# One-core attention with two mixture-of-experts layers: decay sums spread by GpSimd, first block's bias on TensorE, first keys on another queue

## Chip, cores and metric

The kernel runs on 1 core of one Trainium2 chip. The metric is the device time of one execution in microseconds (us), the median of repeated runs. Engines: PE is TensorE (matmuls; PEld its weight loads), DVE is VectorE, ACT is ScalarE, POOL is GpSimd, SP is SyncE. SPq and ACTq are the DMA-issuing instructions of those engines.

## What is computed

Causal attention with a decay bias, then two expert layers, all in fp32:

```python
B, H, S, D = 2, 8, 576, 64
scores = q @ k.T / sqrt(D)
cum = cumsum(log(clip(f, 1e-4, 1)), axis=-1)
scores = where(causal, -1e9, scores + cum[:, :, :, None] - cum[:, :, None, :])
attn = softmax(scores) @ v
x = moe_top1(attn as 1152 rows of 512)
out = moe_top2(x)
```

The query's own sum `cum[..., None]` is the same for a whole row of the softmax and drops out; the kernel adds only the key's part, the negated sum, which every query row (so every partition) needs.

## The kernel before, in words

**Stages.** `phase_a` is the attention with the routing of the first expert layer (to about 132 us of the span), `moe1` and `moe2` are the expert layers, eight experts of two matrices each.

**Units of the attention.** A batch's 576 rows are cut into chunks of 64, 128, 128, 128, 128 rows (CHUNKS, L39). Units are numbered batch times 5 plus chunk; the two 64-row chunks (units 0 and 5) are worked as one unit, 0, with batch 0 in partitions 0 to 63 and batch 1 in 64 to 127. ORDER (L38) is 0, 1, 2, 3, 4, 6, 7, 8, 9. Each unit has four steps, one for each pair of heads, so step n = 0 to 3 is unit 0, 4 to 7 unit 1, 8 to 11 unit 2, 12 to 15 unit 3, 16 to 19 unit 4, 20 to 23 unit 6. `first[i]` and `last[i]` are a unit's first and last step.

**A step (loop at L550).** `qk` writes the scores of two heads into two PSUM banks: three matmuls a head (hi times hi, hi times lo, lo times hi; L255), and for all units but 0 one bf16 matmul a head that puts -1e9 above the diagonal (L258). DVE then adds the decay bias from SBUF (tile WB, or Wd for unit 0), negates and takes the minimum, in one instruction a head and column group (L265), and ACT takes the exponential (L273). Then follow `warm` (1 to 4 filler matmuls of 512 columns in steps 0 to 15, L562), `trans` of the step two before, what is registered as `mid`, `pvmm` of the step three before, the rest of `trans`, and what is registered as `todo`. `at(n, fn)` registers work with a step; `prep` always goes to `mid`.

**`prep(i)`** transposes a unit's keys and queries on PE into a PSUM bank (L214), ACT writes the hi part (L222) and DVE the lo part (L223). For units above 0 the bank is the single one of `ppk`, for keys and queries alike. Unit 1 is prepared whole in step 1, each other unit's keys in step first-4 and its queries in step first-3.

**The decay sums.** `decay` (L112) ends in tile `ncs`: the negated sums, 128 partitions of 72 values, partition (b*8+h)*8+j. ACT's queue writes them to DRAM as `ncum` (L130), and SP's queue reads them back with a partition step of 0, so that all 128 partitions of WB hold them (`load_w`, L196 to L199): seven loads, 4.7 MB into SBUF. Unit 0 has its own way: `bcast_w` (L179) makes 32 small matmuls of a column of the identity with `ncs`, and DVE adds the mask (L189) into Wd, whose off-diagonal blocks `clear_w` set to -1e9.

**Order.** PE and SP run in program order (`manual_schedule`, L1254) in the attention; ACT, DVE and POOL are ordered by the tile scheduler there. In the expert layers all engines run in program order. SP issues q, k, v, WB, zero-fill and weight DMAs from one queue, in order; a DMA whose data or buffer isn't ready holds all behind it.

**Expert 0's second half (`moe1`, L966).** In each of its eight `ffn2` steps f, expert 1's next weight block is split (ACT hi, L813; DVE lo, L821), and in steps 4 and 6 the two row blocks of expert 1's input are transposed and split (`xsplit`, L867 to L874).

Of the kernel before, what the change touches and what calls it, by code (L numbers as in the profile page):

```python
# [18 lines left out]
P = 128  # L19
# [34 lines left out]
def consts(g):  # L54
# [13 lines left out]
    g.mask = g.ap.tile([P, P], F32, tag="mask", name="mask")  # L68
    nc.vector.tensor_scalar(g.mask, mp, 0.0, NEG, op0=ALU.is_gt, op1=ALU.mult)
# [3 lines left out]
    nc.vector.tensor_scalar(g.nid, mp, 0.0, NEG, op0=ALU.is_equal, op1=ALU.mult)  # L73
    g.ones = cp.tile([P, P], BF16, tag="ones", name="ones")
# [37 lines left out]
def decay(g, f):  # L112
    nc, cp = g.nc, g.cp
    W = B * H * S // P
    fl = g.fl
    nc.vector.tensor_scalar(fl, fl, 1e-4, 1.0, op0=ALU.max, op1=ALU.min)
    a = g.ap.tile([P, W], F32, tag="cma", name="cma")
    tot = cp.tile([P, 1], F32, tag="tot", name="tot")
    nc.scalar.activation(a, fl, AF.Ln, accum_out=tot)
    pt = g.ptr.tile([P, 4, P], "pt")  # L120
    nc.tensor.transpose(pt[:W, 0, :], a, g.ident)
    at = g.ap.tile([W, P], F32, tag="at", name="at")
    nc.vector.tensor_copy(at, pt[:W, 0, :])
    po = g.pxx.tile([P, 512], "po")
    nc.tensor.matmul(po[:, :W], g.seg, tot.to_broadcast([P, W]), start=True, stop=False)
    nc.tensor.matmul(po[:, :W], at, g.tri[:W, :W], start=False, stop=True)
    g.nc_sb = cp.tile([P, W], F32, tag="ncs", name="ncs")
    nc.vector.tensor_scalar(g.nc_sb, po[:, :W], -1.0, None, op0=ALU.mult)
    g.ncum = g.dp.tile([B, H, S], F32, tag="ncum", name="ncum")
    nc.scalar.dma_start(bass.AP(tensor=g.ncum.tensor, offset=g.ncum.offset, ap=[[W, P], [1, W]]), g.nc_sb)  # L130
# [5 lines left out]
def phase_a(g, q, k, v, f, wg, noise, out):  # L136
# [3 lines left out]
    qn, kn, vt, WB, Wd = {}, {}, {}, {}, {}  # L140

    def load_qk(i):
        b, c = units[i]
        s0, r = CHUNKS[c]
        for src, dst, nm in ((q, qn, "qn"), (k, kn, "kn")):
            t = ap.tile([P, DM], F32, tag=nm, name=nm, bufs=2)
            for bb, o in ((0, 0), (1, 64)) if i == 0 else ((b, 0),):
                nc.sync.dma_start(t[o:o + r].rearrange("p (h d) -> p h d", h=H), src[bb, :, s0:s0 + r, :].rearrange("h p d -> p h d"))
            dst[i] = t
# [29 lines left out]
    def bcast_w():  # L179
        w = Wd[0]  # L180
        pp = g.psc.tile([P, 4, P], "pw")
        pw = pp.rearrange("p a w -> p (a w)").rearrange("p (h w) -> p h w", h=H)
        for h in range(H):
            for b in range(B):
                o = (b * H + h) * 8
                nc.tensor.matmul(pw[64 * b:64 * b + 64, h, :], g.ident[:, o:o + 1].to_broadcast([P, 64]), g.nc_sb[:, :64], start=True, stop=True)
        for b in range(B):
            m = slice(64 * b, 64 * b + 64)
            nc.vector.tensor_tensor(w[m, :, m], pw[m], g.mask[m, None, m].to_broadcast([64, H, 64]), op=ALU.add)  # L189

    def clear_w():
        w = Wd[0] = ap.tile([P, H, P], F32, tag="Wd", name="W0", bufs=1)
        nc.gpsimd.memset(w[:64, :, 64:], NEG)
        nc.gpsimd.memset(w[64:, :, :64], NEG)
# [9 lines left out]
    def prep(i, half=None):  # L204
# [31 lines left out]
    def qk(i, p):  # L236
# [23 lines left out]
        for hh in range(2):  # L260
            for n, (a0, a1) in enumerate(cols):
# [4 lines left out]
                    out=ts[hh][:r, a0:a1], in0=ps[hh][:r, :a1 - a0], in1=WB[b][:r, h, a0:a1] if i else Wd[0][:r, h, :r], op0=ALU.add, op1=ALU.min,  # L266
# [231 lines left out]
    clear_w()  # L498
# [15 lines left out]
    at(2, load_w, 0, 192, 576)  # L514
    for i in ORDER[1:]:
# [34 lines left out]
    for n in range(len(work) + LAG + 9):  # L550
# [11 lines left out]
        if n < 16:  # L562
# [277 lines left out]
def moe1(g, x_rows, w1, w2, wg2, wn2):  # L840
# [102 lines left out]
    for e in range(E):  # L943
# [356 lines left out]
```

## Time and profile before

| what | us |
|---|---|
| median of 3 runs | 557.39 (556.54 to 559.33) |
| the profiled execution | 556.42 |
| its span, first to last instruction | 554.6 |
| PE busy | 538.9 (97%) |
| DVE busy | 327.4 (59%) |
| ACT busy | 262.4 (47%) |
| POOL busy | 109.3 (20%) |

The profiled execution's own time is 1.8 us more than its span and 1.0 us less than the median. Matmuls are pipelined and their ends are modelled: a busy PE can still be waiting, and one matmul's duration is longer than the distance to the next. A row of the timeline gives start, duration, engine, line, operation, output and inputs, and in brackets how long the engine had been idle and who released it. A row of the chain of waits gives start, duration and what was on the path that ended last.

### The profile page before, as it was taken

What the parts mean: (1) busy time and instruction counts of PE and PEld (TensorE: products, weight loads), DVE (VectorE), ACT (ScalarE), POOL (GpSimd) and SP (SyncE); (2) the same over time, 40 slices, a digit from 0 to 9 for tenths busy, and PEclk for the clock granted to TensorE, in tenths of its full rate; (3) what the DMA queues carried; (4) which work ended last, traced back from release to release, by engine and by line L of the source; (5) the groups of instructions that cost most, each with busy time, mean ns of one, the idle gap of its engine ahead of it and who ended that gap; (6) DMA issues with size and microseconds to landing.
All of it is one profiled execution on the core that took longest, in us unless ns stands there. A gap on an engine that the chain in (4) does not pass through costs nothing.

```text
span 554.6 us, 11866 instructions
## 1 busy us (share of the span) xinstructions
PE 538.9 (97%) x4292; PEld 505.7 (91%) x4292; DVE 327.4 (59%) x1094; ACT 262.4 (47%) x661; POOL 109.3 (20%) x169
## 2 busy tenths in 40 slices
PE   7899999999999999999999999999999999999994
PEld 4577787788989999999999999999999999999993
DVE  4578778875256374233238766757576666666642
ACT  3566767672265455222225445445454545454510
POOL 5010001111000311320223600222213130314032
PEclk9999999999999999999999999999999999999998
DMA  6798979753998856877884299866777667642021
GB/s 147 210 230 232 332 258 262 263 197 109 308 355 285 283 172 219 260 231 247 269 244 146 69 365 372 220 198 203 186 211 216 212 203 211 182 119 64 19 67 44
DMA packets 103874, 116.80 MB, mean 211 GB/s; under 512 B 38205, under 2 KB 73053, under 8 KB 103808
## 3 DMA queue, kind: packets, MB, share of 16 engines
q1 hardware_dynamic: 97136, 99.86, 59.8%
q0 software_dynamic: 6528, 16.06, 8.8%
q8 instruction: 36, 0.59, 0.4%
q14 instruction: 30, 0.25, 0.1%
q10 hardware_dynamic: 144, 0.04, 0.0%
HBM read 91.63 MB, written 25.85 MB: 212 GB/s over the span
## 4 chain that ended last, share of the span: by engine, by line
PE 87%; DVE 5%; DMA 3%; SPq 3%; issue 1%; ACT 1%; POOL 0%; POOLq 0%; ACTq 0%
PE ps L1061 19%; PE py L1072 19%; PE py L907 12%; PE psn L885 5%; PE ps L895 4%; PE sc L255 3%; PE pt L296 3%; PE pv L324 3%; PE pyr L635 2%; PE px L361 2%; PE pv L319 2%; PE pyr L1094 2%; DMA wr<-in_moe_w_dram 2%; PE ps L896 2%; PE pt L1030 1%; PE warm L101 1%
## 5 line engine op out<-in xcount | busy, mean ns | idle before, releaser
L821 DVE TENSOR_TENSOR wlo<-wr,whi 128x512 fp32r<-128x512 f32 x152 | 103.2, 690 | 26.7 <-ACT whi L813 24.2
L1061 PE MATMUL ps<-X,whi 128*128 128x312 f32 (+4 forms) x512 | 110.2, 306 | 0.0
L1072 PE MATMUL py<-H,whi 128*128 128x312 f32 (+4 forms) x512 | 109.7, 305 | 0.0
L813 ACT ACTIVATE whi<-wr 128x512 fp32r<-128x512 f32 x152 | 93.0, 625 | 29.5 <-PE py L1072 22.7
L1061 PEld LDWEIGHTS ps<-X,whi 128*128 128x128 f32 x512 | 83.5, 189 | 0.1
L1072 PEld LDWEIGHTS py<-H,whi 128*128 128x128 f32 x512 | 83.4, 188 | 0.0
L907 PE MATMUL py<-H,wr 128*128 128x192 f32 (+7 forms) x512 | 80.9, 314 | 0.0
L1072 PE MATMUL py<-H,wlo 128*128 128x312 f32 (+4 forms) x256 | 77.4, 302 | 0.0
L1061 PE MATMUL ps<-X,wlo 128*128 128x312 f32 (+4 forms) x256 | 77.4, 302 | 0.0
L907 PEld LDWEIGHTS py<-H,wr 128*128 128x128 f32 x512 | 76.0, 190 | 0.8
L692 POOL DMA_INDIRECT x<-yr,sl x30 | 34.5, 1149 | 132.5 <-ACT Xn L871 45.4
L1097 POOL DMA_INDIRECT out_dram<-ot,tk x24 | 27.4, 1140 | 148.2 <-DVE ot L1096 147.9
L1063 ACT ACTIVATE H<-ps 128x312 fp32r<-128x312 f32 (+4 forms) x64 | 27.2, 424 | 60.3 <-PE ps L1061 60.3
L273 ACT ACTIVATE pr<-t,nmax 128x192 f32<-128x192 f32 (+4 forms) x72 | 41.9, 584 | 25.9 <-DVE nmax L265 25.6
L1065 DVE SCALAR_TENSOR_TENSOR H<-ps,H 128x312 fp32r<-128x312 f32 (+4 forms) x64 | 30.4, 475 | 30.9 <-ACT H L1063 30.9
L1061 PEld LDWEIGHTS ps<-X,wlo 128*128 128x128 f32 x256 | 48.2, 188 | 0.0
L1072 PEld LDWEIGHTS py<-H,wlo 128*128 128x128 f32 x256 | 48.1, 188 | 0.0
L885 PE MATMUL psn<-Xn,wr 128*128 128x192 f32 (+4 forms) x320 | 46.8, 298 | 0.0
L885 PEld LDWEIGHTS psn<-Xn,wr 128*128 128x128 f32 x320 | 44.2, 190 | 0.2
L265 DVE CUSTOM_DVE_ANT_0 t<-sc,WB 128x192 f32<-128x192 f32 (+3 forms) x64 | 28.6, 478 | 6.3 <-PE sc L258 4.2
L895 PE MATMUL ps<-X,whi 128*128 128x480 f32 (+2 forms) x96 | 31.3, 382 | 0.7 <-DVE X L874 0.7
L1047 POOL DMA_INDIRECT pv<-out_dram,tk x21 | 23.1, 1101 | 35.1 <-DMA out_dram<-ot,tk 20.6
(271 smaller groups left out, 818.5 us busy)
## 6 DMA issues: line engine op xcount, KB each, us to landing
wr<-in_moe_w_dram SPq DMA_DIRECT2D x128, 512.0 KB
xs<-z SPq DMA_DIRECT2D x18, 264.0 KB
x<-z SPq DMA_DIRECT2D x16, 258.0 KB
WB<-ncum SPq DMA_DIRECT2D x4, 576.0 KB
out_dram<-z SPq DMA_DIRECT2D x9, 256.0 KB
qn<-in_q_dram SPq DMA_DIRECT2D x8, 256.0 KB
kn<-in_k_dram SPq DMA_DIRECT2D x8, 256.0 KB
x2g<-x SPq DMA_DIRECT2D x3, 628.9 KB
```

What stands on the lines that cost most here:

```text
L265: nc.vector.tensor_tensor_reduce(out=ts[hh][:r, a0:a1], in0=ps[hh][:r, :a1 - a0], in1=WB[b][:r, h, a0:a1] if i else Wd[0][:r, h, :r], op0= ...
L273: nc.scalar.activation(dst, src, AF.Exp, bias=nmax[:r, h:h + 1], scale=-1.0, accum_out=rsum[:r, h:h + 1])
L692: d = nc.gpsimd.indirect_dma_start(out=g.x2, out_offset=bass.IndirectOffsetOnAxis(ap=sl[:T, t, kk:kk + 1], axis=0), in_=yr[:T, t], in_offs ...
L813: self.g.nc.scalar.activation(self.hi[u], self.g.stream.view(self.base + u), AF.Copy)
L821: self.g.nc.vector.tensor_tensor(self.lo[u], self.g.stream.view(self.base + u), self.hi[u], op=ALU.subtract)
L885: nc.tensor.matmul(ps[:, :C], w[:, d, :], X[e][:, d, :], start=d == 0, stop=d == KD - 1)
L895: nc.tensor.matmul(ps[:, :2 * C], hi[:, d, :], X[e][:, d, :], start=d == 0, stop=False)
L907: nc.tensor.matmul(py[dd][:, :C], w[:, dd, :], H[e][:, f, :], start=f == 0, stop=f == KF - 1)
L1061: nc.tensor.matmul(ps[:, :C], w[:, d, :], X[e][:, x, d, :], start=d == 0 and i == 0, stop=d == KD - 1 and i == 2)
L1065: nc.vector.scalar_tensor_tensor(H[e][:, 1, f, :], ps[:, :C], 0.0, H[e][:, 0, f, :], op0=ALU.max, op1=ALU.subtract)
L1072: nc.tensor.matmul(py[dd][:, :C], w[:, dd, :], H[e][:, x, f, :], start=f == 0 and i == 0, stop=f == KF - 1 and i == 2)
L1097: d = nc.gpsimd.indirect_dma_start(out=out, out_offset=bass.IndirectOffsetOnAxis(ap=tok[:T, t:t + 1], axis=0), in_=ot[:T], in_offset=None, ...
```

## The change

- `bcast_w`, `clear_w`, the mask tile and the DRAM tile `ncum` go. For unit 0, `qk` adds the key's sums with four small fp32 matmuls (two heads, two batches) and the mask with two bf16 matmuls straight into the score banks; DVE's L265 adds a tile of zeros instead of Wd.
- `load_w(b)` is one DMA on ACT's queue from 64 partitions of `ncs` to one row (partition 0) of WB. `spread_w` copies a part of that row to all 128 partitions with GpSimd's `partition_broadcast`: four spreads of two heads by 192 columns ahead of step 0, four of two heads by 384 columns in steps 0 to 3, and for batch 1 four of two heads by 576 columns in steps 6, 8, 10 and 12.
- Unit 0's keys are loaded by ACT's queue instead of SP's.
- In `prep`, unit 1's queries are transposed into a bank of `ptr` instead of the single bank of `ppk`; where there are two parts (unit 0's keys), both hi parts are written before the lo parts.
- From unit 2 on, keys are prepared in step first-5 (was first-4) and q and k are loaded in first-9 (was first-8).
- The filler matmuls of steps 12 to 15 go.
- Expert 1's input is transposed in steps 2 and 5 of expert 0's `ffn2` (was 4 and 6).

```diff
@@ consts
-    g.mask = g.ap.tile([P, P], F32, tag="mask", name="mask")
-    nc.vector.tensor_scalar(g.mask, mp, 0.0, NEG, op0=ALU.is_gt, op1=ALU.mult)
...
+    g.far = g.ap.tile([P, P], BF16, tag="far", name="far")
+    nc.vector.tensor_scalar(g.far, mp, 0.0, None, op0=ALU.is_gt)
+    nc.vector.memset(g.far[64:, :64], 1.0)
@@ decay
-    g.ncum = g.dp.tile([B, H, S], F32, tag="ncum", name="ncum")
-    nc.scalar.dma_start(bass.AP(tensor=g.ncum.tensor, offset=g.ncum.offset, ap=[[W, P], [1, W]]), g.nc_sb)
@@ phase_a
+    zero = ap.tile([P, P], F32, tag="zero", name="zero")
+    nc.gpsimd.memset(zero, 0.0)
@@ load_qk
-                nc.sync.dma_start(t[o:o + r]...
+                (nc.sync if i or src is q else nc.scalar).dma_start(t[o:o + r]...
@@ bcast_w, clear_w: removed
-    def load_w(b, c0, c1, h0=0, h1=H):
-        if b not in WB:
-            WB[b] = ap.tile([P, H, S], F32, tag="WB", name="WB", bufs=2)
-        nc.sync.dma_start(WB[b][:, h0:h1, c0:c1], bass.AP(tensor=g.ncum.tensor, ...
+    def load_w(b):
+        WB[b] = ap.tile([P, H, S], F32, tag="WB", name="WB", bufs=2)
+        nc.scalar.dma_start(WB[b][0:1].rearrange("a h s -> a (h s)"), g.nc_sb[64 * b:64 * b + 64])
+
+    def spread_w(b, c0, c1, h0, h1):
+        w = WB[b][:, h0:h1, c0:c1]
+        nc.gpsimd.partition_broadcast(w, w[0:1])
@@ prep
-            pt = (g.ppk if i else g.ptr).tile([P, 4, P], "pk")
+            pt = (g.ppk if i > 1 or i and isk else g.ptr).tile([P, 4, P], "pk")
...
             for hi, lo, pv in parts:
                 nc.scalar.activation(hi, pv, AF.Copy, scale=sc)
+            for hi, lo, pv in parts:
                 nc.vector.scalar_tensor_tensor(lo, pv, sc, hi, op0=ALU.mult, op1=ALU.subtract)
@@ qk
-            if i and a1 == w:
+            if i == 0:
+                for hh in range(2):
+                    for x in range(B):
+                        o, m = (x * H + 2 * p + hh) * 8, slice(64 * x, 64 * x + 64)
+                        nc.tensor.matmul(ps[hh][m, m], g.ident[:, o:o + 1].to_broadcast([P, 64]), g.nc_sb[:, :64], start=False, stop=False)
+                for hh in range(2):
+                    nc.tensor.matmul(ps[hh][:, :P], g.nid, g.far, start=False, stop=True)
+            elif a1 == w:
...
-                    ... in1=WB[b][:r, h, a0:a1] if i else Wd[0][:r, h, :r], ...
+                    ... in1=WB[b][:r, h, a0:a1] if i else zero, ...
@@ the plan
-    bcast_w()
     warm(g, 4, g.psc)
-    load_w(0, 0, 192, 0, 4)
-    load_w(0, 0, 192, 4, 8)
+    load_w(0)
+    for j in range(4):
+        spread_w(0, 0, 192, 2 * j, 2 * j + 2)
...
-    at(2, load_w, 0, 192, 576)
+    for j in range(4):
+        at(j, spread_w, 0, 192, 576, 2 * j, 2 * j + 2)
+    at(4, load_w, 1)
...
-            at(n - 4, prep, i, 0)
+            at(n - 5, prep, i, 0)
             at(n - 3, prep, i, 1)
...
-                at(max(n - 8, 0), load_qk, i)
+                at(max(n - 9, 0), load_qk, i)
...
-        at(first[6] - 9 + 2 * j, load_w, 1, 0, 576, 2 * j, 2 * j + 2)
+        at(6 + 2 * j, spread_w, 1, 0, 576, 2 * j, 2 * j + 2)
...
-        if n < 16:
+        if n < 12:
             warm(g, (4, 4, 4, 2)[n] if n < 4 else 1, g.psc)
@@ moe1
-                if f == (0 if e else 4):
+                if f == (0 if e else 2):
                     xsplit(e + 1, 0)
-                if f == (3 if e else 6):
+                if f == (3 if e else 5):
                     xsplit(e + 1, 1)
```

## Rows read from the trace of the kernel before

**Rows 1.** The page, part 1 (busy time) and the path's shares by engine.

```profile
PE 538.9 (97%) x4292; PEld 505.7 (91%) x4292; DVE 327.4 (59%) x1094; ACT 262.4 (47%) x661; POOL 109.3 (20%) x169
...
PE 87%; DVE 5%; DMA 3%; SPq 3%; issue 1%; ACT 1%; POOL 0%; POOLq 0%; ACTq 0%
```

**Rows 2.** Busy time by stretch: us, PE, PEld, DVE, ACT, POOL, PEclk, DMA, GB/s.

```profile
10.00:20.00 10.00, 7.82 (x59) 4.88 (x58) 5.09 (x23) 4.83 (x19) 0.00 (x0) 1.00 0.76 167
...
40.00:50.00 10.00, 10.00 (x104) 7.62 (x100) 7.99 (x33) 5.76 (x20) 0.00 (x0) 1.00 0.92 249
...
60.00:70.00 10.00, 9.51 (x115) 7.73 (x114) 8.46 (x38) 7.63 (x20) 0.00 (x0) 1.00 1.04 331
```

**Rows 3.** Timeline, the first fillers, keys' DMA, ACT's logarithm, unit 0's key transposes.

```profile
1.07 3.87 PE L101 MATMUL warm<-ones 128*128 128x512 bf16 x10 [1.07 <-DVE ohs L845]
...
2.65 1.32 SPq L148 DMA_DIRECT2D kn<-in_k_dram  x2
...
2.88 0.26 ACT L119 ACTIVATE cma<-fl 128x72 f32<-128x72 f32 x1 [0.84 <-DVE fl L116]
...
6.89 0.63 PE L214 MATMUL pk<-ident,kn 128*128 128x128 f32 x4 [1.02 <-DMA kn<-in_k_dram]
```

**Rows 4.** Timeline, unit 0's bias and its first scores; a later mask pair.

```profile
7.89 1.15 PE L186 MATMUL pw<-ncs,ident 128*64 128x64 f32 x32
...
11.38 1.02 PE L101 MATMUL warm<-ones 128*128 128x512 bf16 x4 [0.77 <-DVE W L189]
...
12.33 0.55 PE L255 MATMUL sc<-kT,qT 64*128 64x128 f32 x6
...
20.30 0.28 PE L258 MATMUL sc<-stri,nid 128*128 128x128 bf16 x2
```

**Rows 5.** Timeline, unit 1's preparation and its first scores; unit 2's.

```profile
15.70 0.66 PE L214 MATMUL pk<-ident,qn 128*128 128x128 f32 x4 [1.41 <-DVE kT L223]
...
19.79 0.58 PE L255 MATMUL sc<-kT,qT 64*128 64x192 f32 x6
...
23.55 0.66 PE L214 MATMUL pk<-ident,qn 128*128 128x128 f32 x4 [0.56 <-DVE kT L223]
```

**Rows 6.** Timeline, PE at 57 to 65 us.

```profile
57.56 1.40 PE L255 MATMUL sc<-kT,qT 64*128 64x288 f32 x12
...
61.34 1.06 PE L255 MATMUL sc<-kT,qT 64*128 64x288 f32 x12
...
65.02 0.33 PE L296 MATMUL pt<-ident,pr 128*128 128x128 f32 x1 [0.49 <-DVE rt L456]
```

**Rows 7.** Timeline, end of expert 0.

```profile
156.58 0.48 PE L895 MATMUL ps<-X,whi 128*128 128x480 f32 x1 [0.68 <-DVE X L874]
```

**Rows 8.** Stretches of one microsecond: issuing from one queue, and later.

```profile
4.00:5.00 1.00, 1.00 (x7) 0.58 (x5) 0.82 (x5) 0.00 (x0) 0.99 (x3) 1.00 0.86 193
...
13.00:14.00 1.00, 1.00 (x7) 0.65 (x6) 0.43 (x4) 0.75 (x4) 0.00 (x0) 1.00 1.07 267
```

**Rows 9.** Timeline, unit 0's hi and lo parts.

```profile
8.43 0.38 ACT L222 ACTIVATE kT<-pk 128x256 fp32r<-128x256 f32 x1 [0.49 <-DVE kT L223]
...
9.34 0.69 DVE L223 SCALAR_TENSOR_TENSOR qT<-pk,qT 128x512 fp32r<-128x512 f32 x1
```

**Rows 10.** Chain of waits, fillers of step 12 and the DVE stretch.

```profile
41.37 0.22 PE warm L101
...
58.36 0.60 DVE kT L223
```

**Rows 11.** Chain of waits, the sums' way through DRAM.

```profile
6.17 3.74 DMA ncum<-ncs
```

**Rows 12.** Timeline, a POOL copy; biases of units 1 and 2.

```profile
4.11 0.63 POOL L229 COPY IW<-ident 128x512 f32<-128x512 f32 x1
...
20.57 0.36 DVE L265 CUSTOM_DVE_ANT_0 t<-sc,WB 128x192 f32<-128x192 f32 x1 [0.25 <-DMA v<-in_v_dram]
...
38.32 0.49 DVE L265 CUSTOM_DVE_ANT_0 t<-sc,WB 128x320 f32<-128x320 f32 x1
```

More of the change, by code (lines that the diff above doesn't have):

```diff
@@ L139, in phase_a @@
     units = [(b, c) for b in range(B) for c in range(5)]
-    qn, kn, vt, WB, Wd = {}, {}, {}, {}, {}
+    qn, kn, vt, WB = {}, {}, {}, {}
+    zero = ap.tile([P, P], F32, tag="zero", name="zero")
+    nc.gpsimd.memset(zero, 0.0)
     def load_qk(i):
@@ L147, in load_qk @@
             for bb, o in ((0, 0), (1, 64)) if i == 0 else ((b, 0),):
-                nc.sync.dma_start(t[o:o + r].rearrange("p (h d) -> p h d", h=H), src[bb, :, s0:s0 + r, :].rearrange("h p d -> p h d"))
+                (nc.sync if i or src is q else nc.scalar).dma_start(t[o:o + r].rearrange("p (h d) -> p h d", h=H), src[bb, :, s0:s0 + r, :].rearrange("h p d -> p h d"))
             dst[i] = t
@@ L177, in clear_v @@
             nc.gpsimd.memset(vz[b], 0.0)
[L179 to L194, printed above, removed]
-    def load_w(b, c0, c1, h0=0, h1=H):
-        if b not in WB:
-            WB[b] = ap.tile([P, H, S], F32, tag="WB", name="WB", bufs=2)
-        nc.sync.dma_start(WB[b][:, h0:h1, c0:c1], bass.AP(tensor=g.ncum.tensor, offset=g.ncum.offset + (b * H + h0) * S + c0, ap=[[0, P], [S, h1 - h0], [1, c1 - c0]]))
+    def load_w(b):
[4 more added lines that the diff above has]
+        nc.gpsimd.partition_broadcast(w, w[0:1])
     kT = [ap.tile([P, B, KD, S], F32R, tag=f"kT{j}", name=f"kT{j}") for j in range(2)]
@@ L254, in qk @@
                     a, bb = ((qh, kh), (qh, kl), (ql, kh))[m]
-                    nc.tensor.matmul(ps[hh][:r, :a1 - a0], a[sl, p, :r], bb[sl] if i == 0 else bb[sl, a0:a1], start=m == 0, stop=m == 2 and (i == 0 or a1 < w))
-            if i and a1 == w:
+                    nc.tensor.matmul(ps[hh][:r, :a1 - a0], a[sl, p, :r], bb[sl] if i == 0 else bb[sl, a0:a1], start=m == 0, stop=m == 2 and a1 < w)
+            if i == 0:
[6 more added lines that the diff above has]
+            elif a1 == w:
                 for hh in range(2):
@@ L265, in qk @@
                 nc.vector.tensor_tensor_reduce(
-                    out=ts[hh][:r, a0:a1], in0=ps[hh][:r, :a1 - a0], in1=WB[b][:r, h, a0:a1] if i else Wd[0][:r, h, :r], op0=ALU.add, op1=ALU.min,
+                    out=ts[hh][:r, a0:a1], in0=ps[hh][:r, :a1 - a0], in1=WB[b][:r, h, a0:a1] if i else zero, op0=ALU.add, op1=ALU.min,
                     scale=-1.0, scalar=nm if n else 3.0e38, accum_out=nm)
@@ L497, in phase_a @@
     decay1(g, f)
-    clear_w()
     load_consts()
```

## The prediction

> **What bounds the kernel now.** I read the page first: PE is busy 97% of the span and carries 87% of the path that ended last [rows 1]. So time comes back where PE waits or does work that nothing needs. The busy time by stretch says where that is: of the 10 us from 10 to 20, PE is busy 7.82, while from 40 to 50 it has no gap [rows 2]. From 60 to 70 PE has a gap again and DVE is at its busiest, 8.46 [rows 2]. The timeline then names the waits. Unit 0's keys arrive at 6.89, after 1.02 us of waiting [rows 3]. Fillers wait 0.77 us for DVE's `W` [rows 4]. Unit 1's queries wait 1.41 us for the lo part of its keys, because both use one PSUM bank, and unit 2's 0.56 us for the same reason [rows 5]. DVE releases PE 0.49 us late at 65.02 [rows 6], and X 0.68 us late at 156.58 [rows 7]. All are PE waits with nothing after them that catches up, so what is saved should reach the end: behind 20 us PE is nearly closed.
>
> **The change part by part.** Gains are positive.
>
> *Keys on ACT's queue.* SP takes 2.65 to 3.97 to issue the two key DMAs, behind the queries [rows 3]. Two queues issue at the same time. With one queue issuing the DMAs move 193 GB/s; later they reach 267 [rows 8]. The 0.55 MB of f, queries and keys takes 2.85 us at the first rate and 2.06 at the second, 0.8 less, but SP's next loads (unit 0's values) now compete. I take 0.5, nearer to the second row than to nothing. The ends: ACT could issue them behind its logarithm, which ends at 3.14; 1.32 of issuing then ends at 4.46 instead of 3.97, a loss of 0.5. Or it issues them at once, and the gain is 1.0. If the two issues stand before the logarithm, that moves from 2.88 by up to 1.3 to 4.2; the transpose that needs it stands behind ten fillers that end at 4.94 [rows 3], so it costs nothing, and without that cover about 1.
>
> *Hi parts before lo parts.* ACT waits 0.49 between the two hi parts of unit 0's keys for DVE's lo part [rows 9]; then DVE's lo parts end 0.5 sooner, and the queries' lo part, which ends at 10.03 [rows 9], too. 0.5; ends 0 and 0.5. With the keys, unit 0's scores can end 1.0 sooner.
>
> *Unit 0's bias on PE.* The 32 matmuls of 1.15 us [rows 4] stood in the time until the queries' lo part is there, so taking them away gives nothing by itself. What counts is the way from that lo part (10.03) to the second step's scores (12.33) [rows 4, 9], 2.30 us: now it is 0.2 for the last two score matmuls (a third of 0.55), four bias matmuls at a thirty-second of 1.15 each (0.14), a mask pair (0.28) [rows 4], and four fillers at 0.22 [rows 10], 1.50 in all. Gain 0.8. The three later steps pay 0.42 each for bias and mask, 1.26. Sum -0.45. Ends: -1.3, if the wait for `W` would have gone anyway; +0.8, if the three payments only take the place of waits. DVE loses two instructions of `W` and keeps L265 with a tile of zeros of the same size.
>
> *Unit 1's queries in another bank.* The wait of 1.41 goes [rows 5]. What is late next is the third step's bias and unit 1's lo parts, all on DVE, which is busy 5.09 of these 10 us [rows 2]: it has room. 1.4; ends 0.7 (half of it taken by DVE) and 1.6. Unit 1's first scores, at 19.79 before [rows 5], then start some 2 us sooner.
>
> *Keys a step sooner.* Unit 2's wait of 0.56 [rows 5] goes, since its lo part is ready two steps ahead: 0.55. In the DVE stretch PE's scores take 1.40 instead of 1.06, and a transpose waits 0.49 [rows 6], 0.83 together; the lo part of unit 6's keys, 0.60 on DVE in the middle of it [rows 10], moves a step ahead. 0.5; ends 0 and 0.8. The DMAs of q and k move a step ahead as well, on SP, past one step's zero-fill.
>
> *Four fillers fewer.* 0.22 each on the path [rows 10], 0.85 for steps 12 to 15; ends 0.3 (DVE, 7.99 of 10 there, takes the place) and 0.9. PE has no gap there and the granted clock is 1.00, the higher level [rows 2]; I expect no fall.
>
> *Expert 1's input sooner.* The two X subtractions come ahead of two weight splits each in DVE's order, so the wait of 0.68 [rows 7] goes and ffn2 itself is the limit. 0.65; ends 0 and 0.7.
>
> *The sums' way to the partitions.* Before, the write to DRAM lands 3.74 us after 6.17, at 9.9 [rows 11]. The DMA to one row takes its place in ACT's queue; I take the same 3.74, so the row is there at 9.9. SP no longer waits for it, and its loads of unit 2 and the values go earlier; no PE wait hung on these. A spread of 2 x 192 columns has no row. The nearest is POOL's copy of 512 columns, 0.63 us [rows 12]: 0.47 for 384 columns; I take that. From below it could hardly be less; from above, the spreads cost nothing until they are late. Unit 1's first bias is due at 20.57 and unit 2's last at 38.32 [rows 12], now some 2.0 and 2.5 us sooner by the terms above, so 18.6 and 35.8. POOL did nothing from 10 to 20 [rows 2]. With c for a spread of 384 columns, the first is done at 9.9+c and the last of unit 2 (four of c, four of 2c) at 9.9+12c: no wait up to c = 2.1 us, four times what I take. 0. The seven loads of WB, 4.7 MB, leave the DMA queues; nothing on the path waits for these, so 0.
>
> The Trainium skill, GPSIMD Engine Reference, section 2.1, says that the first call to a freshly loaded kernel pays about 6 us that no row shows. Estimated by that, unit 1's first spread would be done at 16.4 instead of 10.4 and still ahead of its need at 18.6, so the sum by it is the same, with 2.2 us of cover left.
>
> **The sum.** 0.5 + 0.5 - 0.45 + 1.4 + 0.55 + 0.5 + 0.85 + 0.65 = 4.5 us. The profiled execution took 556.42, so 551.9; the median of the runs is 1.0 above it, so I forecast 552.9. A measurement can tell about 0.5% (2.8 us) from no change: faster means below 554.6, slower above 560.2.
>
> **The rivals.**
>
> *The start is not passed on, 555.7.* ACT issues the keys behind the logarithm (-0.5 in place of 0.5), the lo parts still alternate with the hi parts (0.1), DVE takes half of the query wait (0.7), the DVE stretch gives nothing, the fillers 0.6: -0.5 + 0.1 - 0.45 + 0.7 + 0.55 + 0.6 + 0.65 = 1.7, no measurable change. For it: ACT and DVE are ordered by a scheduler that sees estimates, and DVE is at 8 of 10 from 30 us on. Against it: DVE has half of its time free from 10 to 20. This is also the case in which the change doesn't do what it says.
>
> *The spreads are late, slower.* Place: L265 of units 1 and 2. It begins at c = 2.1; at 2.53 the wait (12 x 2.53 + 9.9 - 35.8 = 4.5) has eaten the gain; from 2.8 on the kernel is slower by over 0.5%; at c = 4 the wait is 22.1 and the time 575.0. Batch 1's spreads (12c more) would be late by then too. For it: no row of this trace shows POOL moving data across partitions, and a fixed cost ahead of the first spread of more than 8.2 us has the same effect on unit 1. Against it: it must be four times as slow as a copy. The same page, section 3.2, has a reduction along the partitions of 128 x 2048 at 247.7 us; by that rate, an estimate of 46 us a spread, the kernel would be slower by hundreds of us; no run here shows whether a spread resembles it.
>
> *More than the sum, 550.5.* Every term at its upper end, the three later payments of bias only in the place of waits: 1.0 + 0.5 + 0.8 + 1.6 + 0.55 + 0.8 + 0.9 + 0.7 = 6.85. For it: PE has 2.18 us of gaps from 10 to 20 [rows 2], more than I take there. Against it: all terms would have to be at their best together.
>
> **How the numbers follow.** The forecast 0.55, its own range 551.2 to 554.6; more than the sum 0.11; not passed on 0.22; late spreads 0.12. Faster 0.66, same 0.22, slower 0.12. The range reaches down to 549.7 (all upper ends, and 0.85 less, the lowest run's distance from the median) and up to 557.2 (not passed on, with X at 0 and the bias at its lower end of -1.3: 555.7 + 0.65 + 0.85), and leaves out the late spreads and little else.
>
> **What would show it.** Right: unit 0's key transposes near 6.4; no wait for kT on unit 1's or 2's query transposes; unit 1's first scores near 17.8; no transpose that waits for DVE near 61; no wait for X before L895; spreads of about 0.5, 0.9 and 1.3 us on POOL. Wrong: L265 waiting for POOL; ACT's DMA issues behind L119; DVE ending the idle time before transposes in steps 1 to 3; a POOL row of several us, or a gap ahead of the first spread that holds unit 1.

## The result, and the profile after

The changed kernel takes 552.6 us (median of 4 runs, 552.13 to 553.31); the kernel before, with one run more than above, takes 557.64 (556.54 to 559.33). The ratio is 0.9896, 95% interval 0.9864 to 0.9929: faster by 1.0%. The profiled execution took 553.04, span 551.3, so 3.4 us less than that of before. Executions of one kernel differ (of 25 of the kernel before on one chip the shortest took 555.5 at a mean granted clock of 0.997, the longest 563.2 at 0.987), so parts are weighed below by the start of steps in the traces too, and not by medians alone.

The page of the changed kernel, busy time and the path by engine (before: [rows 1]):

```profile
PE 538.7 (98%) x4296; PEld 506.0 (92%) x4296; DVE 326.4 (59%) x1093; ACT 261.7 (47%) x661; POOL 119.8 (22%) x180
...
PE 91%; DVE 4%; ACT 2%; issue 1%; DMA 1%; POOL 0%; ACTq 0%; POOLq 0%; DVEq 0%
```

SP's queue is gone from the path (it had 3%). Busy time by stretch, as in [rows 2]:

```profile
10.00:20.00 10.00, 10.00 (x105) 6.78 (x100) 4.52 (x22) 5.02 (x20) 5.99 (x9) 1.00 0.85 169
40.00:50.00 10.00, 9.85 (x97) 7.51 (x95) 8.41 (x32) 7.47 (x23) 0.00 (x0) 1.00 0.65 196
60.00:70.00 10.00, 9.77 (x114) 8.35 (x114) 8.21 (x33) 7.13 (x19) 0.00 (x0) 1.00 1.08 377
```

From 10 to 20 PE has no gap where it had 2.18 us of them. The timeline of the changed kernel shows how (it answers to [rows 3 to 5, 7, 12]; SPq and ACTq are the issuing instructions):

```profile
0.79 1.42 ACTq L149 DMA_DIRECT2D kn<-in_k_dram  x2
...
1.07 4.45 PE L102 MATMUL warm<-ones 128*128 128x512 bf16 x10 [1.07 <-DVE ohs L841]
...
6.28 0.60 PE L201 MATMUL pk<-ident,kn 128*128 128x128 f32 x4
...
6.75 0.54 ACTq L182 DMA_DIRECT2D WB<-ncs  x1
...
7.35 0.37 SPq L149 DMA_DIRECT2D qn<-in_q_dram  x1
...
8.54 0.63 PE L243 MATMUL sc<-kT,qT 64*128 64x128 f32 x4 [0.35 <-ACT qT L209]
...
8.70 0.68 DVE L211 SCALAR_TENSOR_TENSOR qT<-pk,qT 128x512 fp32r<-128x512 f32 x1
...
9.69 0.45 PE L248 MATMUL sc<-ncs,ident 128*64 128x64 f32 x8
10.08 0.28 PE L250 MATMUL sc<-far,nid 128*128 128x128 bf16 x2
10.20 1.03 PE L102 MATMUL warm<-ones 128*128 128x512 bf16 x4
11.15 0.55 PE L243 MATMUL sc<-kT,qT 64*128 64x128 f32 x6
...
13.43 0.53 ACTq L182 DMA_DIRECT2D WB<-ncs  x1
14.00 0.40 ACT L268 ACTIVATE pr<-t,nmax 128x128 f32<-128x128 f32 x1 [5.52 <-DMA v<-in_v_dram]
14.01 9.79 POOL L186 PARTITION_BROADCAST WB<-WB  x11 [6.00 <-issue]
...
16.62 0.58 SPq L149 DMA_DIRECT2D kn<-in_k_dram  x1
...
18.67 0.58 PE L243 MATMUL sc<-kT,qT 64*128 64x192 f32 x6
19.02 0.81 DVE L332 SCALAR_TENSOR_TENSOR rinv<-rsum,one 128x8 f32<-128x8 f32 x1 [0.73 <-ACT pr L268]
...
22.01 0.60 PE L201 MATMUL pk<-ident,qn 128*128 128x128 f32 x4
...
62.09 0.33 PE L291 MATMUL pt<-ident,pr 128*128 128x128 f32 x1 [0.23 <-DVE PT L297]
...
152.18 0.48 PE L891 MATMUL ps<-X,whi 128*128 128x480 f32 x1
```

The waits for `kT` at the queries of units 1 and 2 (at 13.44 and 22.01 now) and the wait for `X` have gone, of the one at 65.02 [rows 6] 0.23 is left (62.09), and no L260 (L265 before) waits for a spread. Some things are not as I thought. `load_w` stands twice in ACT's queue: once ahead of unit 0's hi parts (6.75) and once, at 13.43, ahead of unit 0's first exponential, and the profile has that DMA wait for a load of values on SP. ACT does nothing for 5.52 us, though the first minimum was there at 10.76. Unit 1's first scores start at 18.67, not near 17.8. And unit 3's keys are issued at 16.62, where SP issued them at 22.01 before.

The start of a step's first scores (and of the two expert-layer matmuls `psn` and X) in the profiled execution of each kernel, from the timelines:

| kernel | step 0 | 4 | 8 | 16 | 20 | 35 | psn | X | span |
|---|---|---|---|---|---|---|---|---|---|
| before | 9.94 | 19.79 | 29.50 | 53.43 | 69.36 | 115.91 | 133.36 | 156.58 | 554.6 |
| changed | 8.54 | 18.67 | 27.94 | 51.20 | 66.87 | 112.34 | 129.79 | 152.18 | 551.3 |
| e1 one DMA on SP | 8.48 | 18.61 | 27.20 | 50.44 | 66.10 | 111.56 | 131.04 | 153.57 | 551.3 |
| e2 both on SP | 8.06 | 18.20 | 26.79 | 50.03 | 65.70 | 111.18 | 128.62 | 151.17 | 548.8 |
| e3 one bank | 8.65 | 24.93 | 33.53 | 56.76 | 72.43 | 117.90 | 135.65 | 158.26 | 555.9 |
| e10 = e2, one bank | 8.23 | 20.00 | 28.80 | 52.06 | 67.72 | 113.19 | 130.64 | 153.01 | 550.7 |
| e9 old sums | 9.43 | 20.38 | 33.32 | 56.56 | 72.17 | 117.65 | 135.08 | 157.32 | 554.9 |
| e11 old sums and keys | 9.61 | 17.79 | 27.50 | 54.56 | 70.50 | 117.05 | 139.79 | 163.60 | 561.3 |
| e4 old keys | 8.64 | 18.33 | 29.09 | 52.98 | 68.92 | 115.45 | 132.90 | 155.21 | 552.9 |
| e5 fillers | 8.48 | 18.61 | 27.89 | 51.36 | 67.02 | 112.50 | 130.06 | 152.42 | 550.3 |
| e12 old unit-0 bias | 9.04 | 18.35 | 27.70 | 51.06 | 67.02 | 112.48 | 133.19 | 155.44 | 553.4 |
| e7 keys on SP | 8.90 | 19.03 | 28.29 | 51.54 | 67.21 | 112.68 | 130.38 | 152.86 | 550.6 |
| e6 X late | 8.64 | 18.77 | 28.09 | 51.33 | 67.00 | 112.47 | 129.92 | 153.47 | 551.2 |
| e8 spreads six times | 8.64 | 18.77 | 32.38 | 67.05 | 82.71 | 128.19 | 145.69 | 168.65 | 566.3 |

Kernels whose edit comes later than a step (e5, e6, e8) start steps 0 and 4 within 0.1 us of the changed kernel: differences of that size mean nothing. Ahead of psn the profiled executions of e1, e11 and e12 wait 1.5 to 2.0 us for gathered rows, and those of the others don't; their psn, X and span hold that.

The gain is 1.4 at step 0, 1.6 at step 8, 2.5 at step 20, 3.6 at step 30 and 4.4 at X. After that 1.0 is lost in this execution: from X to the end it takes 399.1, the kernel before 398.1 and the twelve experiments 397.5 to 397.9. The trace has a wait there (at 286.95) that none of the other profiled executions has. Waits of PE from 160 to 320, us, times, longest:

```profile
PE pyr L631 <- DVE l L634: 1.2, 1, 1.2
```

What makes this wait wasn't followed further.

### The profile page after: what moved, and what is told of

It reads as the page before. It is cut to its first block, busy times and chain, and to the rows that moved or that the text cites. A ratio compares the mean times of both kernels' runs of the same rounds, so it can differ in the third digit from the quotient of the medians.

```text
span 551.3 us, 11880 instructions
## 1 busy us (share of the span) xinstructions
PE 538.7 (98%) x4296; PEld 506.0 (92%) x4296; DVE 326.4 (59%) x1093; ACT 261.7 (47%) x661; POOL 119.8 (22%) x180
## 4 chain that ended last, share of the span: by engine, by line
PE 91%; DVE 4%; ACT 2%; issue 1%; DMA 1%; POOL 0%; ACTq 0%; POOLq 0%; DVEq 0%
PE py L1068 20%; PE ps L1057 20%; PE py L903 14%; PE psn L881 7%; PE sc L243 4%; PE ps L891 4%; PE pt L291 3%; PE pyr L631 3%; PE pv L319 2%; PE pyr L1090 2%; PE ps L892 2%; PE pv L314 2%; PE px L356 2%; PE pt L1026 1%; PE pk L201 1%; ACT pr L268 1%
## 5 line engine op out<-in xcount | busy, mean ns | idle before, releaser
L268 ACT ACTIVATE pr<-t,nmax 128x192 f32<-128x192 f32 (+4 forms) x72 | 41.9, 584 | 25.2 <-DVE nmax L260 19.5
L260 DVE CUSTOM_DVE_ANT_0 t<-sc,WB 128x192 f32<-128x192 f32 (+3 forms) x64 | 28.6, 477 | 5.5 <-PE sc L253 3.7
L243 PE MATMUL sc<-kT,qT 64*128 64x288 f32 (+4 forms) x264 | 30.0, 330 | 1.2 <-DVE nmax L260 0.6
```

Of the source, the lines that this page charges most:

```text
L260: nc.vector.tensor_tensor_reduce(out=ts[hh][:r, a0:a1], in0=ps[hh][:r, :a1 - a0], in1=WB[b][:r, h, a0:a1] if i else zero, op0=ALU.add, op1 ...
L268: nc.scalar.activation(dst, src, AF.Exp, bias=nmax[:r, h:h + 1], scale=-1.0, accum_out=rsum[:r, h:h + 1])
```

## The experiments

Each set ran beside the kernel before, whose medians were 557.5 to 557.6; the ratios are to that kernel, with 95% intervals. By them e3, e4, e8, e9 and e11 lie clear of the changed kernel's 0.9864 to 0.9929; the intervals of the others overlap with it, so what is said of those rests on the starts in the table, one execution each. Theories and rivals were written down ahead of the runs. Diffs are shown in part, against the changed kernel.

**e1 and e2: whose queue carries the one-row DMAs.**

```diff
-nc.scalar.dma_start(WB[b][0:1]...
 e1:
+(nc.sync if b else nc.scalar).dma_start(WB[b][0:1]...
 e2:
+nc.sync.dma_start(WB[b][0:1]...
```

> Edit: the changed kernel with batch 1's one-row DMA of the sums on SP's queue instead of ACT's; nothing else. In the changed kernel's trace this DMA stands in ACT's queue ahead of unit 0's first exponential, waits for another DMA until 13.43 and holds ACT from 8.48 to 14.00, though the exponential's input was there at 10.97. Theory A (the hold is on the path): the first exponential moves to about 11.0, unit 1's lo parts end some 2 us sooner, unit 1's first scores start at 18.2 or sooner instead of 18.67, the bias of step 4 no longer waits behind them, and the time falls by 0.5 to 1.0 from the changed kernel's 552.6. Rival B (PE's own order is the limit there): the first exponential moves as well, but unit 1's first scores stay within 0.15 of 18.67 and the time stays within 0.4.

> Edit: both one-row DMAs of the sums on SP's queue. Beside what the run before shows, the first of them takes 0.54 us of ACT's queue from 6.75 on, and unit 0's first hi part starts at 7.34 though its transposes are done near 6.9. Theory A: unit 0's first hi part starts at 6.9 to 7.0, its scores end 0.35 to 0.4 sooner than 9.76, and unit 1's first scores come 0.3 to 0.4 before those of the kernel with one DMA moved; time 0.3 less than that kernel. Rival B: the queries' transposes and fillers fill that time, unit 1's first scores stay within 0.1 of that kernel's.

Measured: e1 551.12 (ratio 0.9877, 0.9815 to 0.9940), e2 550.86 (0.9890, 0.9851 to 0.9930). The timeline of ACT in e1, the first exponential:

```profile
10.74 0.40 ACT L268 ACTIVATE pr<-t,nmax 128x128 f32<-128x128 f32 x1 [2.31 <-DVE nmax L260]
```

and in e2 the first hi parts, 0.48 sooner than in the changed kernel (7.34):

```profile
6.86 0.66 ACT L209 ACTIVATE kT<-pk 128x256 fp32r<-128x256 f32 x2 [3.52 <-PE pk L201]
```

In e1 the exponential waits for its data again and not for a DMA. PE gains nothing from it until step 5 (20.14 against 20.20), then 0.73 by step 6 (22.18 against 22.91): the late exponentials push ACT and DVE back, and PE meets that two steps of unit 1 later. So A's 0.5 to 1.0 is right by the starts (the median, 1.5 lower, gives more than they do), and B is right that unit 1's first scores stay. In its profiled execution e1 lost the gain again in one PE wait of 1.5 us for gathered rows (psn 131.04). e2 adds 0.4 from step 0 on, as its theory A has it: the half microsecond of the hi parts that `load_w` had taken. e2 has the lowest median of all kernels run.

**e3 and e10: the bank of unit 1's queries**, alone, and with ACT's queue free (on top of e2).

```diff
-pt = (g.ppk if i > 1 or i and isk else g.ptr).tile([P, 4, P], "pk")
+pt = (g.ppk if i else g.ptr).tile([P, 4, P], "pk")
```

> Edit: unit 1's queries go back to the single bank of ppk; nothing else. Theory A (the term of the prediction, 1.4 us): the queries' transposes wait 1.2 to 1.6 for the lo part of the keys, unit 1's first scores start 1.2 to 1.6 later than 18.67, the time is 1.2 to 1.6 above the changed kernel. As ACT is held until 14.00 there, the keys' hi part is late and the wait can be up to 3 us: theory A' has unit 1's first scores 2.5 to 3.5 later. Rival B (DVE takes half of it): 0.5 to 0.9 later.

> Both one-row DMAs on SP's queue (the fastest run so far, 550.9), and unit 1's queries back in the single bank of ppk. Theory A: the 5.2 us that the bank cost in the earlier run came from ACT's queue (the one-row DMA of batch 1 holding ACT, so the hi part of unit 1's keys came late) and from the fall of the granted clock behind PE's wait of 3.5 us; with ACT free the wait on the lo part is near the 1.41 of the kernel before, no fall of the clock, and the time is 552.0 to 552.6. Rival B: the single bank alone makes the long wait, whatever the queue: a PE wait over 2.5 us on kT, granted clock 0.50 for some us behind it, 555 to 556.5.

Measured: e3 557.85 (0.9988, 0.9945 to 1.0031), e10 553.4 (0.9937, 0.9901 to 0.9972). So e3 is 5.2 slower than the changed kernel where the prediction's term is 1.4. PE in e3, timeline:

```profile
17.17 1.11 PE L201 MATMUL pk<-ident,qn 128*128 128x128 f32 x4 [3.46 <-DVE kT L211]
18.22 0.90 PE L243 MATMUL sc<-kT,qT 64*128 64x128 f32 x6
```

e3 by stretches of 2 us, columns as in [rows 2] (PEclk is the third number from the end):

```profile
16.00:18.00 2.00, 0.83 (x4) 0.71 (x4) 0.69 (x1) 0.40 (x1) 2.00 (x3) 0.50 0.27 60
18.00:20.00 2.00, 2.00 (x19) 1.55 (x18) 0.69 (x1) 0.60 (x1) 2.00 (x4) 0.50 0.23 55
20.00:22.00 2.00, 2.00 (x7) 0.78 (x5) 0.51 (x4) 0.88 (x4) 2.00 (x3) 0.50 1.11 273
22.00:24.00 2.00, 2.00 (x21) 1.53 (x21) 0.90 (x5) 0.14 (x1) 2.00 (x3) 0.83 0.82 210
```

Waits of PE in e10:

```profile
PE pk L201 <- DVE kT L211: 1.4, 1, 1.4
```

With ACT held until 13.69, the hi part of unit 1's keys is written from 15.83 on and the lo part from 16.43; the queries' transposes, in the same bank, wait 3.46. PE did nothing from 14 to 17, and the granted clock was 0.50, the level of 1.2 GHz, from 16 to 22: six scores take 0.90 where they take 0.55. So unit 1's first scores are 6.3 later (24.93), above theory A' too, which had the wait and not the clock. With ACT free the wait is 1.4, as before [rows 5], the clock stays at 1.00, and from step 2 on PE is 1.8 to 2.0 later than in e2. Of e10 theory A is right on the wait and the clock; its time was 0.8 too low.

**e9 and e11: the sums through DRAM again**, unit 0's bias with them, with keys as changed (e9) and in step first-4 and loads in first-8 as before (e11).

```diff
+    nc.scalar.dma_start(bass.AP(tensor=g.ncum.tensor, ...), g.nc_sb)
...
+    bcast_w()
...
-    load_w(0)
-    ... spread_w(0, 0, 192, ...)
+    load_w(0, 0, 192, 0, 4)
+    load_w(0, 0, 192, 4, 8)
...
+    at(2, load_w, 0, 192, 576)
...
 e11 also:
-            at(n - 5, prep, i, 0)
+            at(n - 4, prep, i, 0)
...
-                at(max(n - 9, 0), load_qk, i)
+                at(max(n - 8, 0), load_qk, i)
```

> Edit: the whole old way of the decay sums (DRAM tile, seven loads on SP's queue, 32 small matmuls and the mask by DVE for unit 0) put back into the changed kernel; keys on ACT's queue, hi before lo, banks, key steps, fillers and X stay as changed. Theory A (the prediction's sum, in which the new way of the sums costs 0.45): the four steps lose 0.6 each of bias and mask on PE, get back the wait for W of 0.8 and the DVE instructions of it, and unit 1's first scores start 0.3 to 1.0 sooner than 18.67; time 0.3 to 1.0 below the changed kernel. Rival B (the new way pays): W, SP's hold until the sums are in DRAM and the 4.7 MB more make unit 1's first scores later than 18.67 and the time 0.5 to 1.5 above. Rival C: no difference within 0.3, the two ways cost the same at the start and nothing later.

> The old way of the decay sums (DRAM tile, seven loads, bias of unit 0 in SBUF), keys in step first-4 and loads in first-8 as before the change; the rest of the change kept (first keys on ACT's queue, hi parts first, the second bank, fewer fillers, expert 1's input sooner). Theory A: what made the old way 6 us dearer in the earlier run was that SP is held until the sums are in DRAM and unit 2's and 3's keys, wanted a step sooner, were waited for, and the clock fell; with the keys a step later neither wait stands, the granted clock stays 1.00, and the kept parts give what they were costed at less what is not passed on: 553.5 to 555.0. Rival B: the old way is slow by itself (SP held until 10, PE waiting for W): 556.5 or more, with a PE wait over 1 us that is not on a key DMA.

Measured: e9 558.84 (1.0024, 0.9979 to 1.0069), e11 558.1 (1.0022, 0.9994 to 1.0051). e9, timeline, and its granted clock behind that:

```profile
11.88 1.26 SPq L148 DMA_DIRECT2D kn<-in_k_dram  x1
...
19.19 0.65 PE L214 MATMUL pk<-ident,kn 128*128 128x128 f32 x4 [1.87 <-DMA kn<-in_k_dram]
...
31.66 0.66 PE L214 MATMUL pk<-ident,kn 128*128 128x128 f32 x4 [2.06 <-DMA kn<-in_k_dram]
```

```profile
20.00:22.00 2.00, 2.00 (x14) 1.30 (x13) 1.10 (x4) 0.48 (x1) 0.00 (x0) 0.50 0.59 134
```

e11, timeline, its granted clock behind that, and two rows of the kernel before:

```profile
21.47 0.51 SPq L199 DMA_DIRECT2D WB<-ncum  x1
...
22.64 2.17 SPq L148 DMA_DIRECT2D kn<-in_k_dram  x1
...
32.12 0.66 PE L214 MATMUL pk<-ident,kn 128*128 128x128 f32 x4 [3.15 <-DMA kn<-in_k_dram]
```

```profile
32.00:34.00 2.00, 1.88 (x18) 1.56 (x20) 0.69 (x3) 0.91 (x2) 0.00 (x0) 1.00 0.55 94
```

```profile
22.01 1.86 SPq L148 DMA_DIRECT2D kn<-in_k_dram  x1
...
30.80 0.60 PE L214 MATMUL pk<-ident,kn 128*128 128x128 f32 x4
```

In e9 theory A, with its gain, was wrong. Rival B was right that unit 1's first scores come later than 18.67 (20.38), but the loss is 6.2 and not 0.5 to 1.5: PE waits 1.87 and 2.06 for the keys of units 2 and 3, and from 20 to 26 the clock is at 0.50. Of e11 both theories fell. The time is B's, but the wait is on a key DMA and that for `W` was 0.6: with the later keys unit 2's wait goes (step 4 starts at 17.79, the earliest of all, step 8 at 27.50), and then PE stands 3.15 us for unit 3's. SP issues them behind the 1.5 MB of WB at 22.0 in the kernel before and 22.2 and 22.6 here, and they are there at 31.7 and 32.1; before, PE reached their transposes at 30.80 and found them there without a wait. The packets of the traces show what holds them: in the kernel before the 1024 packets of 1536 bytes that make up those 1.5 MB started from 22.05 to 28.00, and from 23.5 to 27.0 not one of 256 bytes, the size of those of q, k and v; in e11 it is 22.67 to 28.88, and none from 24.0 to 27.5. That is the point: the old way of the sums sets a date before which unit 3's keys can't be had, and the kernel before ran behind it. What is made faster ahead of it turns into that wait. (In e11's profiled execution 5.3 more are lost from step 35 to psn, with a fall of the clock to 0.50; the starts up to step 35 don't hold that.)

**e4: keys a step later, alone.**

```diff
-            at(n - 5, prep, i, 0)
+            at(n - 4, prep, i, 0)
...
-                at(max(n - 9, 0), load_qk, i)
+                at(max(n - 8, 0), load_qk, i)
```

> The changed kernel with unit 2's and later keys prepared in step first-4 and q and k loaded in first-8 again, as before the change. The prediction put 0.55 (unit 2's query wait) and 0.5 (DVE stretch) on this part, 1.05 us. Theory A, from the two traces: 1.05 to 1.7 slower than the changed kernel's 552.6, 553.7 to 554.3, of it about 0.5 between steps 8 and 10 and 0.6 or more between steps 20 and 30 (units 7 to 9, where the changed kernel gained 0.64 that no term held). Rival B: PE is closed from step 8 on, so the order of the keys is worth nothing alone: 552.6 within 0.4, every step from 9 on within 0.3 us of the changed kernel.

Measured: 554.72 (0.9962, 0.9950 to 0.9974), 2.1 slower. Timeline of PE in e4:

```profile
23.14 0.66 PE L201 MATMUL pk<-ident,qn 128*128 128x128 f32 x4 [1.33 <-DVE kT L211]
```

The loss is above both theories. Unit 2's queries wait 1.33, not 0.56 [rows 5]: PE gets there 1.18 sooner than before (21.81 and 22.99), the lo part is there only 0.41 sooner. By step 10 1.9 is lost and by step 30 3.2, 1.1 of it after step 20.

**e5: the fillers of steps 12 to 15.**

```diff
-        if n < 12:
+        if n < 16:
```

> The changed kernel with one filler matmul in each of steps 12 to 15 again. The prediction's term: 0.85 slower, 553.4. Theory A, from the traces (steps 11 to 16 gained about 0.5 on the kernel before, and in part of that stretch the ACT and DVE chain is what PE waits for): 0.3 to 0.6 slower, 552.9 to 553.2, granted clock unchanged at 1.00. Rival B: DVE is the bound there, so the fillers fit in waits: no difference, step 16's start within 0.15 us of the changed kernel.

Measured: 551.85 (0.9908, 0.9890 to 0.9926). Step 16's first scores in e5, against 51.20 in the changed kernel:

```profile
51.36 0.93 PE L243 MATMUL sc<-kT,qT 64*128 64x288 f32 x10
```

That is 0.16 for four fillers, 0.27 by psn: rival B, or nearly. Steps 13, 14 and 15 start 0.15, 0.36 and 0.57 later than in the changed kernel, so each filler delays PE by its 0.21 at first; by step 16 all but 0.16 is gone. That the median lies below the changed kernel's may be the loss of 1.0 behind X, which e5's profiled execution doesn't have; no run shows it.

**e12: unit 0's bias the old way, the spreads kept.**

```diff
+    bcast_w()
     warm(g, 4, g.psc)
     load_w(0)
-            if i == 0:
...
-            in1=... if i else zero
+            in1=... if i else Wd[0][:r, h, :r]
```

> The changed kernel with unit 0's bias the old way (32 small matmuls, mask added by DVE into the tile W, L265's second operand W instead of zeros); the spreads and all other parts are kept. Theory A, the prediction's term of -0.45 taken back with the 0.60 a step that the trace shows for bias and mask in place of 0.42: without them three later steps gain 1.8 in all, the first step loses what it waits for W (0.8 or more, as the other way was costed): 0.5 to 1.0 faster than the changed kernel, 551.6 to 552.1, with steps 4 and 8 starting 0.5 to 1.0 sooner. Rival B: the second step's fillers wait longer for W now that the queries are there sooner, and the payments of 0.60 only fill waits of the third and fourth steps: no gain, 552.4 to 553.5, step 4 within 0.3 us of the changed kernel or later.

Measured: 553.66 (0.9928, 0.9888 to 0.9968). Timeline of PE and DVE in e12:

```profile
8.18 1.39 DVE L187 TENSOR_TENSOR W<-pw,mask 64x512 f32<-64x512 f32 x2 [2.25 <-PE pw L184]
...
10.40 0.33 PE L257 MATMUL sc<-kT,qT 64*128 64x128 f32 x2 [0.91 <-DVE kT L225]
...
12.22 0.55 PE L257 MATMUL sc<-kT,qT 64*128 64x128 f32 x6
```

Unit 0's second step is 1.07 later, its fourth 0.08 later, steps 4 and 8 are 0.32 and 0.24 sooner, step 16 0.14, and by step 20 it is 0.15 later. Theory A missed, and rival B by little: there is a small gain, gone 50 us on. DVE's two `W` instructions, 1.39, stand ahead of the lo parts, so PE waits 0.91 for `kT`, which neither theory held; the three later steps, 0.4 to 0.5 shorter each without bias and mask on PE, win 1.39 from there to step 4.

**e7: keys on SP's queue.**

```diff
-(nc.sync if i or src is q else nc.scalar).dma_start(
+nc.sync.dma_start(
```

> The changed kernel with unit 0's keys on SP's queue again, behind the queries. The prediction's term: 0.5 slower, 553.1, ends -0.5 and 1.0. Theory A, from the traces (keys landed 0.9 sooner, the transposes began 0.6 sooner, the rest was held by the decay chain and fillers): unit 0's key transposes 0.3 to 0.6 later and all steps behind them by as much, 552.9 to 553.2. Rival B: what is late next is the one-row DMA ahead of ACT's hi part and the queries' lo part, so step 1's scores do not move: 552.6 within 0.2.

Measured: 552.37 (0.9915, 0.9871 to 0.9959). Timeline of PE in e7, against 6.28:

```profile
6.71 0.79 PE L201 MATMUL pk<-ident,kn 128*128 128x128 f32 x4
```

All steps are 0.33 to 0.37 later, as A has it; the medians can't tell that.

**e6: expert 1's input late.**

```diff
-                if f == (0 if e else 2):
+                if f == (0 if e else 4):
...
-                if f == (3 if e else 5):
+                if f == (3 if e else 6):
```

> The changed kernel with expert 1's input transposed in steps 4 and 6 of expert 0's second half again. The prediction's term: 0.65 slower, 553.3. Theory A, from the traces (first scores of the second expert layer to X gained 0.83): 0.7 to 0.9 slower, with a PE wait of 0.6 to 0.8 for X, and the steps of the attention unchanged. Rival B: the time behind expert 1 takes it back (some executions of the changed kernel lose 1.1 at 280 us), so the median stays within 0.3 of 552.6.

Measured: 555.31 (0.9951, 0.9914 to 0.9989; the ten runs go from 552.58 to 558.98). Waits of PE in e6:

```profile
PE ps L891 <- DVE X L870: 1.0, 1, 1.0
```

X starts 1.29 later, psn 0.13 later: 1.16 for this part, above theory A. The median, 2.7 above the changed kernel's, is further off than the part explains; why stays open.

**e8: late spreads, made on purpose.**

```diff
+        for _ in range(1 if b else 6):
         nc.gpsimd.partition_broadcast(w, w[0:1])
```

> Each of batch 0's eight spreads six times over (the same values), all else as the changed kernel: the rival of late spreads made true. In the changed kernel's trace the first spread starts at 14.0, behind 6.0 us in which GpSimd does nothing, and a spread of 384 columns takes 0.54 from one to the next, one of 768 columns 0.92. Theory A (the rival's mechanism with its threshold): the spreads of unit 2's four steps are done at 32.5, 38.0, 43.5 and 49.0, the last needed at 34.9: DVE's L265 (L260 here) waits for GpSimd, some 10 to 14 us in all, 563 to 570 with a fall of the clock if PE stands idle. Rival B: GpSimd and DVE share more than the data, and DVE's work under the spreads is slowed so that the price is above that, over 572. Rival C: the scheduler or the cover hides it: below 556.

Measured: 571.13 (568.21 and 574.06; ratio 1.0218, 1.0120 to 1.0316). Waits of DVE from 0 to 80 in e8:

```profile
DVE t L261 <- POOL WB L187: 14.1, 4, 6.8
```

The wait is A's upper figure, 14.1, and the time, of two runs, 1 us above A's range: step 12 starts 15.9 later than in the changed kernel, and the granted clock was 0.50 from 27 to 33 and from 47 to 53, behind two of PE's three waits (2.39 and 5.46). Unit 2's waits came in front of its first and third step (4.8 and 6.8), not one in each as I had worked out; why, wasn't followed.

## Why the prediction came out right, and where its steps did not

The forecast of 552.9 stands 0.3 from the median, and the waits that it was made of are the ones that went. But several terms have the wrong size, and two misses cancel: that it came so near is in part luck.

- *Sum.* 4.5 was forecast on the profiled execution; 4.4 was there at X, 3.4 at the end, after the wait behind X. And the median, which I put 1.0 above the profiled execution, lies 0.4 below it. These two misses cancel.
- *Unit 1's queries in another bank*, 1.4: 1.8 to 2.0 (e10). While ACT is held by `load_w` it is worth over 5 (e3), since the wait is 3.46 and the clock falls.
- *Keys a step sooner*, 1.05: 2.1 to 3.1 (e4, median and psn). The mechanism was right; the size was read from waits of before, and those grow when PE comes sooner and the DVE chain does not.
- *Fillers*, 0.85: 0.2 (e5). I had taken the end at which PE is the limit; it was the other end, at which ACT and DVE take the place. PE busy 10.00 of 10 [rows 2] hid that, since fillers count as busy.
- *X*, 0.65: 0.83 against before, 1.16 in e6. *Keys on ACT's queue*, 0.5: 0.35 (e7), behind the decay's own matmuls. *Hi before lo*, 0.5: ACT's gap of 0.49 went, and the queries' lo part ends 0.65 sooner (9.38) though the first hi part starts only 0.22 sooner, since `load_w` stands ahead of it and takes 0.4 (e2). No run takes this part back alone.
- *Unit 0's bias*, -0.45: -0.3 at step 4, +0.15 from step 20 on (e12), the latter hardly more than the 0.1 that means nothing. Bias and mask cost 0.51 a step (9.69 to 10.20), not 0.42: I took the 32 rows of L186 [rows 4] for 32 matmuls, as the section on the kernel before does, but its loops make 16, each two rows in fp32, so four are eight rows, 0.29 by that row and 0.39 measured, not 0.14; the mask pair takes 0.12 to the next row where I had put its whole length, 0.28. The way from the queries' lo part to the second step's scores is 1.77 (9.38 to 11.15), not 1.50. And DVE's 1.39 of `W` ahead of the lo parts, which the change takes away, I didn't count.
- *The sums' way, 0.* The step that failed is "no PE wait hung on these". For the spreads it holds: batch 0's eight take 5.93 us together (e1), where I took 12 x 0.47 = 5.64, all twelve are done by 25.2, no instruction waits for them, and e8 shows the rival's wait, in its place, once they take six times as long. But SP's release and 4.7 MB less are what the other terms rest on: with the old way step 35 starts 5.3 (e9) and 4.7 (e11) later than in the changed kernel, and by the medians the gain is gone, whichever way the keys go (unit 0's bias, taken back with it, counts 0.3 at most by e12). A cost of nothing was right for the kernel before and wrong for the kernel with the other six edits.
- *Left out:* what stands in ACT's queue behind the one-row DMAs. I wrote that the DMA takes the place of the old one in ACT's queue, and didn't name batch 1's, which a scheduler put ahead of unit 0's exponentials: 0.75 (e1), plus 0.4 (e2).

The measured sizes don't add up to the gain. Taken back one at a time, the bank (5.6), the sums' way (5.3, e9), the keys' step (3.1), X (1.2), the keys' queue (0.3) and the fillers (0.2) cost 15.7 by the starts, where all of them together gave 4.4 at X: the parts lean on each other, and a list of separate gains, as the prediction has it, can't show that. Of the rivals, late spreads and more than the sum didn't come about; "not passed on" was true of unit 1's first scores (1.1 sooner, not 2) and of the fillers.

## What to carry to other kernels

Before a transfer is costed at nothing, work out the date before which it, and what its queue holds behind it, can't be there, and set that beside the date at which the consumer will come once the other edits work. A DMA put on a compute engine's queue has to be named with what stands behind it there and with what it may wait for. And a PE that is busy with fillers isn't a PE that limits: take one away and look whether the next real matmul starts sooner.

## What the runs showed of the hardware

- Ahead of the first spread GpSimd does nothing for 5.93 to 6.87 us in every kernel that has spreads, and for 6.8 to 9.1 us again before the next iota; the kernels without spreads have no such gap between a copy and that iota. The Trainium skill, GPSIMD Engine Reference, section 2.1, puts the first call of a freshly loaded kernel at about 6 us without a row; the trace agrees. It was covered here: unit 1's need came at 20.5, the spread was there at 14.7.
- A spread of 384, 768 and 1152 columns takes 0.67, 1.05 and 1.42 us by its row, and the next starts 0.54 or 0.91 behind one of the first two: far from the 46 us of the prediction's rival.
- The small DVE instruction L332 (its line in the changed kernel), both of whose operands are in SBUF, took 0.81 us at 19.02 under the spreads, against 0.17 at most in the kernel before. It ends with the spread under which it starts. Of 14 such cases in all kernels 13 end 0.12 us before the spread's row does, however long that takes (0.21 to 0.87); in the 14th, in e8, only 0.17 of the spread was left. The bias instruction L260, with one operand in PSUM, takes 0.35 to 0.36 for 192 columns under spreads and elsewhere. The Trainium skill, SBUF — State Buffer, in its part on the two separate sides, says that a DVE instruction with two SBUF inputs and one of GpSimd that reads SBUF exclude each other for a whole instruction; the traces agree. A spread and L332 in the changed kernel, then in e2, then in e7:

```profile
18.90 1.05 POOL L186 PARTITION_BROADCAST WB<-WB  x1
19.02 0.81 DVE L332 SCALAR_TENSOR_TENSOR rinv<-rsum,one 128x8 f32<-128x8 f32 x1 [0.73 <-ACT pr L268]
```

```profile
17.39 1.05 POOL L186 PARTITION_BROADCAST WB<-WB  x1
18.04 0.28 DVE L332 SCALAR_TENSOR_TENSOR rinv<-rsum,one 128x8 f32<-128x8 f32 x1 [0.74 <-ACT pr L268]
```

```profile
18.82 1.05 POOL L186 PARTITION_BROADCAST WB<-WB  x1
19.54 0.21 DVE L332 SCALAR_TENSOR_TENSOR rinv<-rsum,one 128x8 f32<-128x8 f32 x1 [0.74 <-ACT pr L268]
```

- PE idle for 1.87 us in e9 was followed by a granted clock of 0.50 from 20 to 26, 3.46 us in e3 by 0.50 from 16 to 22 and 2.39 in e8 by 0.50 from 27 to 33, while 3.15 in e11, 2.06 in e9 and 2.37 in e8 were followed by 1.00. What tells these apart no run here shows.
